# Which engine splits which block of two MLPs, the order of a Strassen product, and the PSUM banks of second layers

## The chip, the core and the metric

The program runs on one core of a Trainium2 chip. The metric is device time in microseconds (us) of one execution, as the median of three. TensorE (PE) does the matrix products; its weight loads are listed as PEld. VectorE (DVE), ScalarE (ACT) and GpSimd (POOL) do everything on elements; SyncE (SP) issues the transfers. Each engine works off its own queue in order. PE writes into PSUM, the others read it there, except GpSimd, which works on SBUF alone.

## The reference, cut to what matters

```
attn = clustered_attention(q, k, v, centroids)      # 2 batches, 8 heads, 768 tokens, 64 wide
x = attn.transpose(0, 2, 1, 3).reshape(1536, 512)
h = x @ w_in                  # first MLP, w_in 512 x 2048
g = h * sigmoid(h)
x = g @ w_out                 # 2048 x 512
gate = sigmoid(x @ w_gate)    # second MLP, w_gate and w_val 512 x 1536
val = x @ w_val
out = (gate * val) @ w_out2   # 1536 x 512
```

All is float32. Each operand of an MLP product is kept as a high and a low part, and a product is three PE products: high by high, high by low, low by high. The low part of a block is the block minus its high part.

## The kernel before

**Stages.** The attention over four pairs of heads in each of two batches takes roughly the first 275 us. The first MLP follows in N1 = 8 layers of 256 hidden columns, the second in N2 = 6. A layer of the first MLP makes its hidden block (`hidden`, "first layer" product) and adds that block times its rows of `w_out` to `acc` (`mixed`). A layer of the second MLP makes gates and values (`gated`) and adds their product times `w_out2` (`out_of`).

**One Strassen product.** `strassen` (L700) makes a 2 x 2 block product from seven half-size products, named by letters: x, y, w, z, and then X (accumulated onto x's bank), v and W (accumulated onto w's bank). It gives four result blocks: block (1,1) from u3 and w once z is done, block (0,0) from X, block (1,0) from v, block (0,1) from W. Here the first number (m) is the half of the hidden columns and the second (h) the half of the tokens. x and w sit in PSUM pool `ppa`, y, z and v in `ppb`; each pool has two banks, and a bank is handed on when its reader is done. v is the product of a22 with the operand t4.

**What follows each block.** In `hidden`, ACT applies Silu (L783), ACT writes the high part (`gha`, L61), and an engine subtracts for the low part (`gla`, L760 in `split`): GpSimd for h = 0, VectorE for h = 1. In `gated`, ACT makes the gate by Sigmoid (L835); the value block is multiplied by its gate (L841), then split into `ghb` and `glb`. In all layers of the second MLP but the last, GpSimd multiplies blocks (1,1) and (1,0) and subtracts for blocks (0,0) and (1,0); in the last layer VectorE does it all.

**The order of the work.** PE's order is that of the program text (`manual_schedule` for PE, L925). One step of `strassen` is one product. The loop (L940, L961) issues x and y of the next layer, then the second-layer product of the layer before, then the remaining five products. So PE's steady order is: w z X v W, next x, next y, second-layer product (`y_00None` to `y_21None`, or `z`), w z and so on; in the second MLP seven gate products and seven value products take the place of the seven. All other engines' orders are laid down by a planner, which walks a simulated timeline and prefers the ready instruction that stands earlier in the program text. Weight conversions stand early there: they are traced when `weights` first reaches two jobs ahead.

**Banks of second layers.** A second-layer product has six bank-size parts; `third` (L690) puts parts 0, 1, 3, 4 into `ppb` and parts 2, 5 into `ppa`. In the first and last `out_of` and in single-batch `mixed` the parts alternate.

**Weight conversions.** Each 128 x 512 block of weights takes ACT L597, POOL L598, and on VectorE L599, L600 and L601; then ACT and POOL split it (L61, L609), with POOL sums L636 to L639 for Strassen's operands.

**Start and middle.** Layer 0 of the first MLP is done per batch: `hidden(0, ONE[0])` by Strassen for batch 0, and `hidden_directly(0, 1)` without Strassen for batch 1 (products `p`), while `sums` (L82 to L100) makes the right-hand operands t1 to t4 for batch 1. Layer 0 of the second MLP is done directly for both batches (`gated_directly`, products `q` and `r`), and `sums` and `last` make the Strassen operands of the second MLP's input (tiles `yt`).

Of the kernel before, what the change touches and what calls it, by code (L numbers as in the profile page):

```python
# [15 lines left out]
ALU = mybir.AluOpType  # L16
# [15 lines left out]
def clustered_attention_then_two_mlps(ctx, tc, qT, kT, v, cen, w1i, w1o, w2g, w2v, w2o, out):  # L32
    nc = tc.nc
# [25 lines left out]
    def cast(eng, o, i):  # L59
        if eng is nc.scalar:  # L60
            return nc.scalar.activation(o, i, AF.Copy)  # L61
        if eng is nc.gpsimd:
            return nc.gpsimd.tensor_scalar(o, i, 1.0, 1.0, op0=ALU.mult, op1=ALU.mult)
        return nc.vector.tensor_copy(o, i)  # L64
# [14 lines left out]
    def right_quarter(name, b, q, caster, subber):  # L79
        right_operand(name, b, q, quarters(b)[q], caster, subber, "t1" if q == "12" else None)  # L80
# [21 lines left out]
    def right_last(name, b, src, caster, subber):  # L102
        right_operand(name, b, "t1", src, caster, subber)

    rp = ctx.enter_context(tc.tile_pool(name="rp", bufs=2))
    with ExitStack() as att:
# [182 lines left out]
        for j, (r, o) in enumerate(((L, U), (U, L))):  # L289
# [5 lines left out]
            last = dma(km[r, j].bitcast(F32), kl[r].bitcast(F32))  # L295
# [242 lines left out]
        for n in range(len(tiles) + LAG):  # L538
            if n < len(tiles):
                p, j, i = tiles[n]  # L540
# [42 lines left out]
    ppa = ctx.enter_context(tc.tile_pool(name="ppa", bufs=2, space=PSUM))  # L583
    ppb = ctx.enter_context(tc.tile_pool(name="ppb", bufs=2, space=PSUM))

    N1, N2 = M1 // 2, M2 // 2
# [91 lines left out]
    def weights(*key):  # L678

        n = place[key]  # L680
        for c in range(n, min(n + AHEAD + 1, len(jobs))):
            if c not in made:
                with tc.issue_after(ends[0].ins) if c > AHEAD else nullcontext():
                    made[c] = jobs[c]()
        return made[n]

    def bank(name, pool=None):
        return (pool or ppb).tile([P, 2, NB], F32, tag="o", name=name)

    def third(n, free=False):  # L690
        if free:
            return (ppa, ppb)[n % 2]
        return ppa if n % 3 == 2 else ppb

    def temporary(name):
        return up.tile([P, 2, HS], F32, tag="u", name=name)

    ALL = slice(0, B)

    def strassen(w, name, take, bs, order="xywzXvW"):  # L700

        def run(o, a, q, start=True):
            for k in range(KQ):
                for n, (s, t) in enumerate(((0, 0), (0, 1), (1, 0))):
                    for b in range(B)[bs]:
                        nc.tensor.matmul(  # L706
                            o[:, b, 0:HS],
                            lhsT=w[a][s][:, k, :],
                            rhs=right[b, q][t][:, k, :],
                            start=start and k == 0 and n == 0,  # L710
                            stop=k == KQ - 1 and n == 2,
                            skip_group_check=not start,
                        )
            return o[:, bs, 0:HS]

        name += f"_{bs.start}"
        add = partial(nc.vector.tensor_tensor, op=ALU.add)
        o, c = {}, {}

        def column(n):  # L720
            c[n] = temporary(f"{name}{n}")[:, bs]
            return c[n]

        for n in order:
            if n == "x":
                o[n] = bank(f"{name}x", ppa)
                nc.scalar.activation(column("u2"), run(o[n], "a11", "11"), AF.Copy)
            elif n == "y":
                add(c["u2"], run(bank(f"{name}y"), "s2", "t2"), c["u2"])
            elif n == "z":  # L730
                add(column("u3"), run(bank(f"{name}z"), "s3", "t3"), c["u2"])
            elif n == "w":
                o[n] = bank(f"{name}w", ppa)
                q = run(o[n], "s1", "t1")
            elif n == "X":
                take(run(o["x"], "a12", "21", start=False), 0, 0, bs, False)
            elif n == "v":
                nc.vector.tensor_tensor(
                    c["u3"], c["u3"], run(bank(f"{name}v"), "a22", "t4"), op=ALU.subtract
                )  # L740
                take(c["u3"], 1, 0, bs, True)
            else:
                run(o["w"], "s4", "22", start=False)
                add(c["u2"], q, c["u2"])
                take(c["u2"], 0, 1, bs, True)
            if "w" in o and "u3" in c and "d" not in c:
                add(column("d"), q, c["u3"])
                take(c["d"], 1, 1, bs, True)
            yield
# [3 lines left out]
    def split(src, m, at, i, subber):  # L753

        for t in "hl":
            if (i, m, t) not in gs:
                gs[i, m, t] = gp.tile([P, 2, B, HS], R32, tag=f"g{t}{m}", name=f"g{t}{i}_{m}")
        hi, lo = (gs[i, m, t][(slice(None), *at)] for t in "hl")
        cast(nc.scalar, hi, src)
        subber.tensor_tensor(lo, src, hi, op=ALU.subtract)  # L760
# [16 lines left out]
            take(o[:, :, 0:HS], m, b)  # L777
            yield

    def hidden(i, bs, order="xywzXvW"):  # L780
        def take(c, m, h, bs, inside):
            g = c if inside else temporary(f"g{i}_{m}{h}{bs.start}")[:, bs]
            nc.scalar.activation(g, c, AF.Silu)  # L783
            split(g, m, (h, bs), f"a{i}", nc.gpsimd if h == 0 else nc.vector)

        yield from strassen(weights("1i", i), f"h{i}", take, bs, order)

    def hidden_directly(i, b):
        def take(c, m, b):
            g = temporary(f"g{i}_{m}_{b}")  # L790
            nc.scalar.activation(g, c, AF.Silu)
            split(g, m, (slice(0, 2), b), f"a{i}", nc.vector)

        yield from direct(weights("1i", i), f"p{i}", take, b)
# [35 lines left out]
    def gated(i, bs):  # L830
        gates = {}

        def gate(c, m, h, bs, inside):
            g = c if inside else temporary(f"g2{i}_{m}{h}{bs.start}")[:, bs]
            nc.scalar.activation(g, c, AF.Sigmoid)  # L835
            gates[m, h] = g

        def value(c, m, h, bs, inside):
            g = gates[m, h]
            beside = nc.gpsimd if i < N2 - 1 else nc.vector  # L840
            (beside if inside and m else nc.vector).tensor_tensor(g, c, g, op=ALU.mult)  # L841
            split(g, m, (h, bs), f"b{i}", beside if h == 0 else nc.vector)

        yield from strassen(weights("2g", i), f"g{i}", gate, bs)
        yield from strassen(weights("2v", i), f"v{i}", value, bs)

    def gated_directly(i, b):
        gates = {}

        def gate(c, m, b):  # L850
            gates[m] = temporary(f"g2{i}_{m}_{b}")
            nc.scalar.activation(gates[m], c, AF.Sigmoid)

        def value(c, m, b):
            g = gates[m]
            nc.vector.tensor_tensor(g, c, g, op=ALU.mult)
            split(g, m, (slice(0, 2), b), f"b{i}", nc.vector)

        yield from direct(weights("2g", i), f"q{i}", gate, b)
        yield from direct(weights("2v", i), f"r{i}", value, b)  # L860
# [35 lines left out]
    def steps(main, beside=iter(()), n=None):  # L896

        for _ in main:
            next(beside, None)
            if n is not None:  # L900
                n -= 1
                if n == 0:
                    return

    def run(gen):
        for _ in gen:
            pass
# [4 lines left out]
    def plain_operands(name, b):  # L912
        for q in ("11", "21", "12", "22"):
            right_quarter(name, b, q, ACT, DVE)
            yield

    def sums(name, b):
        return right_sums(temporary, name, b, ACT, DVE, kept)

    def last(name, b):  # L920
        right_last(name, b, kept.pop(b), ACT, DVE)

    ONE = [slice(b, b + 1) for b in range(B)]

    order = tc.manual_schedule(engines={mybir.EngineType.PE})  # L925
# [3 lines left out]
        right_quarter("x", 1, q, POOL, POOL)  # L929
    for q in ("21", "22"):  # L930
        right_quarter("x", 1, q, ACT, DVE)
    run(hidden(0, ONE[0], "xwyXzvW"))
    beside = sums("x", 1)
    steps(hidden_directly(0, 1), beside)
    run(beside)
    last("x", 1)
    run(mixed(0, 0))
    run(mixed(0, 1))
    run(hidden(1, ALL))
    for i in range(2, N1):  # L940
        following = hidden(i, ALL) if i < N1 - 1 else hidden(i, ONE[0], "xyXzwvW")
        steps(following, n=2 if i < N1 - 1 else 4)
        run(mixed(i - 1))
        run(following)
    run(hidden(N1 - 1, ONE[1]))
    run(mixed(N1 - 1, 0))
    beside = plain_operands("y", 0)
    steps(mixed(N1 - 1, 1), beside)
    run(beside)
    beside = plain_operands("y", 1)  # L950
    steps(gated_directly(0, 0), beside)
    run(beside)
    beside = sums("y", 0)
    steps(gated_directly(0, 1), beside)
    run(beside)
    run(sums("y", 1))
    last("y", 0)
    last("y", 1)
    run(out_of(0))
    run(gated(1, ALL))  # L960
    for i in range(2, N2):  # L961
        following = gated(i, ALL)
# [57 lines left out]
```

## Time and profile before

| | before |
|---|---|
| median of 3 runs | 893.11 us (892.16 to 893.66) |
| the profiled execution | 893.1 us, span 891.3 us, mean granted TensorE clock 0.959 |
| PE busy | 809.5 us (91%) |
| DVE busy | 644.4 us (72%) |
| POOL busy | 407.9 us (46%) |
| ACT busy | 387.5 us (43%) |
| chain that ended last | PE 55%, DVE 23%, POOL 12%, issue 3%, ACT 3%, DMA 3% |

The profiled execution's time lies 1.8 us over its span and agrees with the median. Busy shares are means over unlike stages: the question is always which wait ends last just before PE goes on. The chain of work that ended last is followed back from the last instruction and says which engine held the end at each moment.

### The profile page before, as it was taken

To read this page: it belongs to the slowest core of one execution; us is meant where nothing else is said; L and a number is where in the kernel's file an instruction comes from. 1 tells how busy PE (TensorE), PEld (TensorE's weight loads), DVE (VectorE), ACT (ScalarE), POOL (GpSimd) and SP (SyncE) were. 2 spreads that over 40 slices of the span, in tenths; PEclk is the share of its full clock that TensorE was granted. 3 is DMA by queue.
4 is the path that set the end of the run, shared out by engine and by line. 5 is a ranking of instruction groups with operands and counts; after the bars stand their busy time and mean duration, and the time that the engine had idled before them with its cause. 6 is when DMAs were issued, how large, how long until landed. Compare 5 with 4: busy or idle time off the path is not lost.

```text
span 891.3 us, 12033 instructions
## 1 busy us (share of the span) xinstructions
PE 809.5 (91%) x4592; PEld 701.4 (79%) x4592; DVE 644.4 (72%) x824; ACT 387.5 (43%) x667; POOL 407.9 (46%) x358
## 2 busy tenths in 40 slices
PE   6899999999998998898898999998979799797987
PEld 4777777777677997787777889997968779686886
DVE  5778877887996988665666669994665858758453
ACT  3456556555675572432514326554424314243030
POOL 3511360581444684534626335552665726558100
PEclk7899999999999999999999999999989999898998
DMA  7564465356321123112111212201210112201003
GB/s 213 143 161 109 113 163 137 89 148 166 108 66 39 57 95 105 41 67 71 47 48 48 71 47 71 96 24 48 71 68 28 71 48 72 71 25 48 1 1 141
DMA packets 25042, 72.10 MB, mean 81 GB/s; under 512 B 4100, under 2 KB 4184, under 8 KB 24984
## 3 DMA queue, kind: packets, MB, share of 16 engines
q1 hardware_dynamic: 24984, 71.33, 26.9%
q8 instruction: 36, 0.59, 0.3%
q14 instruction: 22, 0.18, 0.1%
HBM read 47.87 MB, written 3.19 MB: 57 GB/s over the span
## 4 chain that ended last, share of the span: by engine, by line
PE 55%; DVE 23%; POOL 12%; issue 3%; ACT 3%; DMA 3%; SPq 0%; ACTq 0%; POOLq 0%; DVEq 0%
PE z L879 11%; PE s L412 5%; PE v L452 5%; PE t L444 3%; DVE nm L420 3%; PE g_0w L706 2%; DVE acc L800 2%; PE pm L149 2%; PE y_01None L820 2%; PE y_21None L820 2%; POOL glb L760 2%; PE y_20None L820 2%; PE y_11None L820 2%; PE y_10None L820 2%; PE h_0w L706 2%
## 5 line engine op out<-in xcount | busy, mean ns | idle before, releaser
L425 ACT ACTIVATE e<-s,nm 128x768 f32<-128x768 f32 x96 | 86.5, 902 | 66.8 <-DVE nm L420 65.7
L879 PE MATMUL z<-wu,ghb 128*128 128x512 f32 x288 | 96.9, 420 | 11.5 <-ACT ghb L61 11.5
L420 DVE TENSOR_REDUCE nm<-s 128x1 f32<-128x768 f32 x96 | 90.8, 949 | 11.9 <-PE s L412 9.2
L879 PEld LDWEIGHTS z<-wu,ghb 128*128 128x128 f32 x288 | 58.6, 206 | 26.1 <-ACT ghb L61 14.0
L452 PE MATMUL v<-ph,vv 128*64 128x256 f32 x576 | 75.6, 388 | 0.9 <-DVE xf L464 0.6
L879 PE MATMUL z<-wu,glb 128*128 128x512 f32 x144 | 61.3, 426 | 15.4 <-POOL glb L760 10.9
L800 DVE TENSOR_TENSOR acc<-z,acc 128x1024 f32<-128x1024 f32 x30 | 36.7, 1224 | 41.1 <-PE z L879 41.1
L412 PE MATMUL s<-ka,qa 128*128 128x384 f32 x192 | 59.6, 392 | 6.0 <-ACT e L425 6.0
L444 PE MATMUL t<-ident,e 128*128 128x128 f32 x384 | 58.4, 281 | 2.6 <-ACT ph L61 1.6
L452 PEld LDWEIGHTS v<-ph,vv 128*64 128x64 f32 x576 | 37.8, 136 | 23.9 <-issue 5.9
L412 PE MATMUL s<-k,q 128*128 128x384 f32 x192 | 51.8, 351 | 1.0 <-DVE k L329 1.0
L444 PEld LDWEIGHTS t<-ident,e 128*128 128x128 f32 x384 | 45.3, 144 | 8.5 <-ACT ph L61 1.9
L879 PEld LDWEIGHTS z<-wu,glb 128*128 128x128 f32 x144 | 29.4, 204 | 25.0 <-POOL glb L760 13.3
L412 PEld LDWEIGHTS s<-ka,qa 128*128 128x128 f32 x192 | 29.9, 195 | 20.9 <-ACT e L425 12.5
L350 POOL TENSOR_SCALAR qq<-qq 128x768 f32<-128x768 f32 x7 | 6.1, 874 | 82.5 <-DMA qq<-in_qT 67.2
L439 PE MATMUL u<-ident,e 128*128 128x128 f32 x192 | 36.7, 281 | 0.2 <-DVE ph L64 0.2
L61 ACT ACTIVATE ph<-t 128x512 f32<-128x512 f32 x48 | 28.6, 596 | 19.0 <-PE t L444 18.7
L412 PEld LDWEIGHTS s<-k,q 128*128 128x128 f32 x192 | 35.3, 194 | 1.6 <-DVE k L329 1.5
L482 POOL TENSOR_TENSOR acc<-xf,rb 128x768 f32<-128x768 f32 x7 | 12.8, 1826 | 52.0 <-DVE xf L464 35.1
L464 DVE TENSOR_TENSOR xf<-v,other 64x256 f32<-64x256 f32 x48 | 20.1, 418 | 22.1 <-ACT other L461 21.9
L64 DVE COPY ph<-t 128x512 f32<-128x512 f32 x48 | 32.6, 679 | 4.7 <-PE t L444 4.6
L64 DVE COPY ph<-u 128x512 f32<-128x512 f32 x48 | 32.5, 678 | 3.1 <-PE u L439 3.1
(635 smaller groups left out, 2254.9 us busy)
## 6 DMA issues: line engine op xcount, KB each, us to landing
ri<-in_w1i SPq DMA_DIRECT2D x16, 512.0 KB, 3.2
ro<-in_w1o SPq DMA_DIRECT2D x16, 512.0 KB, 3.1
ka<-kh SPq DMA_DIRECT2D x32, 192.0 KB, 3.9
rg<-in_w2g SPq DMA_DIRECT2D x12, 512.0 KB, 3.1
rv<-in_w2v SPq DMA_DIRECT2D x12, 512.0 KB, 3.1
ru<-in_w2o SPq DMA_DIRECT2D x12, 512.0 KB, 3.2
qq<-in_qT SPq DMA_DIRECT2D x8, 384.0 KB, 4.7
kk<-in_kT SPq DMA_DIRECT2D x8, 384.0 KB, 5.5
```

The costliest lines, as they stand in the source:

```text
L61: return nc.scalar.activation(o, i, AF.Copy)
L64: return nc.vector.tensor_copy(o, i)
L412: nc.tensor.matmul(s[:, g, 0:HS], lhsT=a[:, j, i * P : (i + 1) * P], rhs=c[:, j, g * HS : (g + 1) * HS], start=n == 0, stop=n == 1,)
L420: nc.vector.tensor_reduce(nm, s[:, :, 0:HS], axis=AX.XY, op=ALU.max, negate=True)
L425: nc.scalar.activation(e, s[:, :, 0:HS], AF.Exp, bias=nm, scale=1.0, accum_out=tots[p][:, n : n + 1])
L439: nc.tensor.transpose(both[:, kt - 4, i % GT, :], e[:, kt * P : (kt + 1) * P], ident)
L444: nc.tensor.transpose(t[:, kt, :], e[:, kt * P : (kt + 1) * P], ident)
L452: nc.tensor.matmul(o[(L, U)[kt % 2]], lhsT=vv[:, j, kt, :], rhs=ph[:, kt, :], start=kt < 2, stop=kt >= NT - 2,)
L706: nc.tensor.matmul(o[:, b, 0:HS], lhsT=w[a][s][:, k, :], rhs=right[b, q][t][:, k, :], start=start and k == 0 and n == 0, stop=k == KQ - 1 ...
L800: nc.vector.tensor_tensor(z, o, z, op=ALU.add)
L820: nc.tensor.matmul(o[:, d, 0:width], lhsT=s[:, d, k, :], rhs=t[:, c], start=k == 0 and m == 0, stop=k == 1 and m == 2,)
L879: nc.tensor.matmul(o[:, a, :], lhsT=s[:, q * P : (q + 1) * P], rhs=r, start=k == 0 and m == 0, stop=k == 1 and m == 2,)
```

## The change

- `third`: parts 0 and 3 of a second-layer product go to `ppa`, the other four to `ppb`.
- The Strassen order "xywzXvW" becomes "xywzvXW": v stands before X. At layer 0's batch 0, "xwyXzvW" becomes "xwXyzvW", and the first half of `hidden_directly(0, 1)` stands before its last product W.
- `hidden`: GpSimd subtracts for block (1,1) alone, VectorE for the other three.
- `gated`: GpSimd multiplies and subtracts for block (1,1) alone, VectorE for the others, in every layer.
- Between the MLPs: `sums` and `last` of batch 0 stand ahead of `gated_directly(0, 1)`, those of batch 1 behind it.

```diff
     def third(n, free=False):
         if free:
             return (ppa, ppb)[n % 2]
-        return ppa if n % 3 == 2 else ppb
+        return ppb if n % 3 else ppa
...
-    def strassen(w, name, take, bs, order="xywzXvW"):
+    def strassen(w, name, take, bs, order="xywzvXW"):
...
-    def hidden(i, bs, order="xywzXvW"):
+    def hidden(i, bs, order="xywzvXW"):
         def take(c, m, h, bs, inside):
             g = c if inside else temporary(f"g{i}_{m}{h}{bs.start}")[:, bs]
             nc.scalar.activation(g, c, AF.Silu)
-            split(g, m, (h, bs), f"a{i}", nc.gpsimd if h == 0 else nc.vector)
+            split(g, m, (h, bs), f"a{i}", nc.gpsimd if m and h else nc.vector)
...
         def value(c, m, h, bs, inside):
             g = gates[m, h]
-            beside = nc.gpsimd if i < N2 - 1 else nc.vector
-            (beside if inside and m else nc.vector).tensor_tensor(g, c, g, op=ALU.mult)
-            split(g, m, (h, bs), f"b{i}", beside if h == 0 else nc.vector)
+            eng = nc.gpsimd if m and h else nc.vector
+            eng.tensor_tensor(g, c, g, op=ALU.mult)
+            split(g, m, (h, bs), f"b{i}", eng)
...
-    run(hidden(0, ONE[0], "xwyXzvW"))
+    front = hidden(0, ONE[0], "xwXyzvW")
+    steps(front, n=6)
+    following = hidden_directly(0, 1)
+    next(following)
+    run(front)
     beside = sums("x", 1)
-    steps(hidden_directly(0, 1), beside)
+    next(beside)
+    steps(following, beside)
     run(beside)
...
-    beside = sums("y", 0)
-    steps(gated_directly(0, 1), beside)
-    run(beside)
+    run(sums("y", 0))
+    last("y", 0)
+    run(gated_directly(0, 1))
     run(sums("y", 1))
-    last("y", 0)
     last("y", 1)
```

## Rows read from the trace of the kernel before

**Rows 1.** Waits of PE from 277 us on: total us, times, longest us.

```profile
PE y_00None L820 <- POOL gla L760: 15.8, 5, 3.4
PE z L879 <- ACT ghb L61: 11.5, 5, 2.7
PE z L879 <- POOL glb L760: 10.9, 4, 2.9
PE h_0w L706 <- DVE acc L800: 6.6, 5, 1.3
PE g_0w L706 <- DVE acc L800: 5.3, 4, 1.3
PE z L879 <- DVE glb L760: 4.5, 2, 3.4
PE h_0w L706 <- DVE h_0d L747: 2.3, 1, 2.3
PE h_0y L706 <- ACT ci L597: 1.6, 1, 1.6
```

**Rows 2.** Chain that ended last, around `mixed(4)`: start us, us, work.

```profile
443.99 2.48 POOL gla L760
446.51 3.43 PE y_00None L820 x8
...
452.70 2.72 PE y_10None L820 x12
...
464.90 2.35 PE h_0w L706 x12
467.25 2.08 PE h_0z L706 x12
```

**Rows 3.** Stretches of 2 us in `out_of(4)`: PE busy, granted clock, DMA.

```profile
821.60:823.60 2.00, 1.97 (x5) 0.50 0.00 0
...
825.60:827.60 2.00, 2.00 (x11) 1.00 0.00 0
```

**Rows 4.** Whole layers, first and second MLP: busy PE, PEld, DVE, ACT, POOL; clock.

```profile
446.51:484.06 37.55, 32.83 (x157) 28.93 (x157) 23.69 (x25) 12.56 (x19) 17.42 (x17) 0.95 0.17 57
...
712.04:766.99 54.95, 48.39 (x240) 43.76 (x240) 37.00 (x38) 17.60 (x26) 31.64 (x29) 0.93 0.17 58
```

**Rows 5.** Timelines of ACT, DVE and POOL, first MLP's layer 5: start us, us.

```profile
477.66 0.83 ACT L61 ACTIVATE gha<-h_0u 128x768 fp32r<-128x768 f32 x1
...
474.40 2.32 DVE L601 SCALAR_TENSOR_TENSOR ci<-ri,ci 128x512 int32<-128x512 int32 x1
...
481.49 2.51 POOL L760 TENSOR_TENSOR gla<-h_0u,gha 128x768 fp32r<-128x768 f32 x1
```

**Rows 6.** Chain that ended last, `out_of(3)`.

```profile
766.99 17.03 PE z L879 x67
```

**Rows 7.** Tiles `glb` and line 841 by form: duration ns minimum, median, maximum.

```profile
L760 DVE TENSOR_TENSOR glb<-g_0d,ghb x5: 950/2550/2556, 646.4 to 864.7; 128x768 fp32r<-128x768 f32 x5
...
L841 POOL TENSOR_TENSOR g_0d<-v_0d,g_0d x4: 2034/2042/2228, 642.9 to 808.4; 128x768 f32<-128x768 f32 x4
```

**Rows 8.** Timeline of DVE, values of the second MLP's layer 2.

```profile
697.97 1.17 DVE L599 TENSOR_SCALAR cu<-cu 128x512 int32<-128x512 int32 x1
...
699.92 1.47 DVE L600 SCALAR_TENSOR_TENSOR cu<-ru,cu 128x512 int32<-128x512 int32 x1
701.43 2.22 DVE L601 SCALAR_TENSOR_TENSOR cu<-ru,cu 128x512 int32<-128x512 int32 x1
```

**Rows 9.** Timeline of PE, `out_of(5)`.

```profile
867.45 0.74 PE L879 MATMUL z<-wu,ghb 128*128 128x512 f32 x2 [1.60 <-ACT ghb L61]
```

**Rows 10.** Timeline of DVE, between the MLPs.

```profile
583.54 0.95 DVE L87 TENSOR_TENSOR yt<-acc 128x768 f32<-128x768 f32 x1
...
621.56 0.96 DVE L729 TENSOR_TENSOR g_0u<-g_0y,g_0u 128x768 f32<-128x768 f32 x1 [11.51 <-PE g_0y L706]
```

**Rows 11.** Timeline of DVE, start of the first MLP.

```profile
303.37 2.04 DVE L760 TENSOR_TENSOR gla<-g,gha 128x768 fp32r<-128x768 f32 x1
```

## The prediction

> **What bounds the kernel now.** Start with PE's busy share: at 91% it looks full, so the question is what the other 9% is and whether the 91% runs at full clock. From 277 us on, the list of PE's waits answers the first half [rows 1]: 58.5 us in 27 waits, and nearly all have one of two shapes. The first lies at the start of each second-layer product: PE stops for a low part that GpSimd still makes (`gla`, five times, 3.4 us the longest; in the second MLP first for the high part `ghb`, then for `glb`). The second stands at the next product w: nine times 1.3 us for VectorE's read of the last part (`acc`, L800), that is, for a PSUM bank. The chain that ended last shows both as links on the path [rows 2]: GpSimd's subtraction, then the product, then w. The reader should also see what follows the first wait: eight matmuls take 3.43 us where twelve take 2.72 otherwise, so 1.6 us go to slow matmuls. The granted clock says why: 0.50 after such a wait (1.2 GHz), 1.00 four us later (2.4 GHz) [rows 3]. In `out_of(3)` 67 matmuls take 17.03 us instead of 67 x 2.72 / 12 = 15.2: 1.8 us lost the same way [rows 2, 6]. So a wait of about 3 us costs nearly 5.
>
> Whole layers confirm it. Work per layer is 7 products of 2.08 us and 72 matmuls of 2.72 / 12 us, 14.56 + 16.32 = 30.88 us, where the layer takes 37.55: 6.67 lost. In the second MLP 14 x 2.08 + 16.32 = 45.44 against 54.95: 9.51 lost [rows 2, 4]. VectorE is busy 23.7 of the 37.55 and 37.0 of the 54.95, GpSimd 17.4 and 31.6 [rows 4]: neither is full on average; what counts is order.
>
> **Why the first block is late.** Block (1,0) comes from v. ACT has its high part at 477.66 + 0.83 = 478.49, but GpSimd, whose queue holds weight work in front, begins the subtraction at 481.49 and takes 2.51 us [rows 5]. VectorE does the same in 0.95 us when undisturbed [rows 7].
>
> **The change, part by part.** All sums are against the profiled 893.1 us (span 891.3 and 1.8 around it), which agrees with the median 893.11.
>
> *Banks.* With parts 0 and 3 in `ppa`, w follows part 3 in its pool, not part 5; part 3 is read two parts (5.4 us) earlier, so the wait of 1.3 us goes. w took 2.35 us, not 2.08, after it [rows 2], so each of the nine waits is worth about 1.6: 5 x 1.6 = 8.0 in the first MLP; the four in the second lie inside the 9.51. In return part 0 now needs w's bank, so it waits for VectorE's L744, and z, v and the parts keep `ppb`, whose readers are done sooner.
>
> *First MLP.* GpSimd loses two subtractions per layer and gains (1,1), which is ready four products before the second-layer product starts; VectorE gains one on balance, about 0.95 us in 30.9, and v comes 2.08 us earlier. The five waits (15.8), four slow starts (4 x 1.6 = 6.4) and the five bank waits (8.0) are 30.2 us. What is late next? I laid out VectorE's queue from v's end with one conversion in it, as now. The second-layer product starts 4 x 2.08 = 8.3 us after v. L738, the last conversion step (2.32 contended [rows 5]), two subtractions and L744 at 0.95 are 6.1 us plus about 1 of waiting for ACT: it fits, with some 1.2 us to spare. The other new wait is X. Its bank goes to the next x, which used to start two products after X and now starts one product after: ACT has 2.08 us for a Silu of 0.8 that may stand behind another Silu or high part. Bounds 0 to 2.5 us per layer; I take 0.5, near the rows of ACT, whose steps are 0.8 each [rows 5], for six layers: 3.0. Gain 27.2.
>
> *Second MLP, layers 1 to 4.* Upper bound 4 x 9.51 = 38.0. VectorE gains two instructions on balance (L841 and L760 of (1,0), L760 of (0,0), less L760 of (1,1)). Here VectorE is tighter. Between v's end and the next x lie 2 x 2.08 = 4.16 us, and in them it must do L738, L841 of (1,0) and L841 of (0,0), 2.85 us. But a conversion runs there now: 1.17 + 1.47 + 2.22 = 4.86 us [rows 8]. If its first two steps come in front of X's reader, 2.85 + 2.64 = 5.5, so the next x waits 1.4 us; then L601, two subtractions and L744 end about 0.8 us after the second-layer product could start. That is 2.2 us per layer, with bounds 0 (no conversion in front) and 5.4 (both subtractions at the contended 2.55 [rows 7] as well). I take 2.2, since the planner put that conversion there in this trace, and 0.3 for X's bank between gates and values (ACT, five layers): 8.8 + 1.5 = 10.3. Gain 27.7. GpSimd's two instructions for (1,1), 2.04 [rows 7] and at most 2.51 us [rows 5], start four products before they are needed first and are wanted only in the fourth part: covered; without that cover they would cost what they cost now.
>
> *Last layer.* No next x and y cover its blocks. Its two waits are 1.6 for `ghb` [rows 9] and 1.1 (4.5 less 3.4) for `glb` [rows 1], and 1.8 for the clock: 4.5. After the change (0,0), from X, comes last: L841, high part, L760 is about 2.7 us after X, while W covers 2.08. So 0.7 to 1 stays: gain 3.4, bounds 2 to 4.5.
>
> *Between the MLPs.* In `out_of(0)` PE waits 3.4 us for VectorE's `glb` [rows 1], plus 1.8 of clock. VectorE there runs the sums of both batches from 583.54 on, ahead of batch 1's values, though it is idle 11.5 us later before 621.56 [rows 10]. Putting batch 0's sums first and batch 1's behind the values moves work into that hole. Gain 4.5, bounds 0 and 5.2.
>
> *Start.* X in place of y fills part of the 1.6 us wait at y (one half-size product, 1.0), and the first direct product covers the 2.3 us wait at W: 3.3. But the second part of batch 1's `gla` is only done at 303.37 + 2.04 [rows 11], because VectorE is behind with sums; if that doesn't move, PE waits there instead. I take 1.5, bounds -2 and 3.3.
>
> Sum: 27.2 + 27.7 + 3.4 + 4.5 + 1.5 = 64.3; 893.1 - 64.3 = **828.8**, forecast 829 us. With every new wait at zero: 893.1 - (30.2 + 38.0 + 4.5 + 5.2 + 3.3) = 811.9.
>
> **Rivals.**
>
> *VectorE and GpSimd in each other's way.* The row of `glb` on VectorE has a minimum of 0.95 and a median of 2.55 us [rows 7], so a subtraction here can cost 1.6 more when GpSimd works at the same time. The change gives VectorE more of them. At 2.55 for both moved ones, the first MLP loses 2 x 1.6 less the 1.2 to spare, 2.0 per layer, and the second 3.2: 829 + 5 x 2.0 + 4 x 3.2 = **852**. For it: the row; and (1,1)'s work on GpSimd falls into the same window. Against: GpSimd does less there than before. The Trainium skill, page "SBUF — State Buffer", section "Who interferes with whom", says that a VectorE instruction with two SBUF inputs contends with a GpSimd instruction that reads SBUF, and whoever comes second is held for the whole of the other. The doubled row fits that, and by that rule this rival is the one to expect whenever a weight instruction of GpSimd starts first.
>
> *The moved work doesn't come earlier.* The change is meant to have the blocks ready in time, but the planner may leave the moved subtractions behind conversions, so that the wait at the second-layer product keeps its length under VectorE's name. Then the banks (8.0 + 4 x 1.6), the last layer, the middle and the start are left: 893.1 - 14.4 - 9.4 = **869**. Against: VectorE's totals leave room [rows 4].
>
> *Slower.* X's bank becomes the stop. Place: the next x in the second MLP, and part 0's bank behind L744 in the first. With one conversion at its long durations and L841 at 2.55, X's reader ends 0.95 + 4.86 + 2.55 + 0.95 = 9.3 us after v against 4.16: a wait of 5.15, with the clock 6.95, still under 9.51. It decides with a second conversion in the same window: 6.95 + 4.86 = 11.8, over 9.51; in the first MLP 0.95 + 9.72 + 5.1 + 0.95 = 16.7 against 8.3, with the clock 10, over 6.67. Then 893.1 + 4 x 2.3 + 5 x 3.3 - 9.4 = **909**. Against: the rows show one conversion in that window [rows 8].
>
> **How the numbers follow.** Forecast 829: 0.68, its own range 812 to 843. Port rival 852: 0.17. Work not earlier, 869: 0.08. Slower, 909: 0.05. No change: 0.02. The range to hold 8 in 10 runs from 812 to 857: it takes in the forecast and most of the port rival and leaves out the rest. A measurement of this kernel can tell about 0.2% (1.8 us) from no change. Faster 0.93, same 0.02, slower 0.05.
>
> **What would show it.** Right: no wait of PE for GpSimd's `gla` or `glb`; no wait of w for `acc`; layers of about 31.4 and 48 us; clock 1.00 through second-layer products; new short waits of x for ACT in the first MLP and for L841 in the second, about 0.5 and 1.4 us. Wrong: a wait of `y_00None` or `z` of over 2 us for VectorE's L760 or L744 with the clock at 0.50 behind it, VectorE subtractions at 2.55 throughout, or batch 1's `gla` holding up the first `mixed`.

## The result and the profile after

The changed kernel takes 834.75 us (median of four, 832.95 to 835.97) where the kernel before takes 893.28: a ratio of 0.9345 (95% interval 0.9325 to 0.9366), that is, 6.5% faster. The forecast was 829 us. In a second run of the changed kernel the ratio was 0.9349 (0.9331 to 0.9368). The profiled execution took 835.97 us, span 834.2. One execution of one kernel below (X ahead of v in the value product) took 1975.92 us; its ratio is that of the other three.

PE's waits from 277 us on, in the changed kernel (us in total, times, longest), against [rows 1]:

```profile
PE z L879 <- DVE glb L760: 7.0, 4, 2.0
PE g_0x L706 <- DVE g L841: 5.1, 4, 1.8
PE y L820 <- DVE gla L760: 3.3, 2, 2.5
PE y_00None L820 <- DVE gla L760: 1.6, 2, 0.9
PE h_1w L706 <- DVE h_1d L747: 1.4, 1, 1.4
PE z L879 <- ACT ghb L61: 0.3, 1, 0.3
PE h_0x L706 <- ACT h_0u L727: 0.2, 1, 0.2
```

No wait names GpSimd any more, and none names `acc`; 58.5 us (59.0 with two waits of 0.3 and 0.2 us that [rows 1] leave out) have become 18.9. The largest two are new ones, both on VectorE in the second MLP. Whole layers (first and second MLP; columns as in [rows 4]):

```profile
365.30:396.24 30.94, 30.94 (x158) 28.12 (x157) 26.02 (x26) 12.80 (x20) 17.13 (x16) 1.00 0.20 69
717.75:766.55 48.80, 46.05 (x241) 42.55 (x241) 37.42 (x41) 17.16 (x26) 29.32 (x28) 1.00 0.19 65
```

In a steady layer of the first MLP PE is busy for all of 30.94 us: the bare work was 30.88, so nothing is left to gain there. In the second, 48.80 us stand against 45.44 of bare work. The granted clock is 1.00 in both. The chain that ended last shows the same; the first two lines answer [rows 2], the last (of `out_of(2)`) answers [rows 6]:

```profile
443.67 2.10 PE h_0w L706 x12
...
458.25 2.74 PE y_00None L820 x12
...
666.87 1.49 DVE glb L760
668.35 1.42 DVE g_0u L841
669.77 1.41 DVE glb L760
671.22 16.16 PE z L879 x70
```

w follows the second-layer product without a gap and takes 2.10 us instead of 2.35; twelve matmuls of `y_00None` take 2.74 us, no slow ones among them; 70 matmuls of z take 16.16, that is 0.23 us each, where 67 took 17.03. What is left on the chain is three VectorE instructions in a row in front of z.

Where the time went, from the starts of PE's products in the two timelines (us):

| stretch | before | after | difference | forecast |
|---|---|---|---|---|
| attention, to the first product of the first MLP | 269.7 | 267.7 | -2.0 | 0 |
| from there to `mixed(1)` | 62.2 | 62.8 | +0.6 | -1.5 |
| `mixed(1)` to `mixed(6)` | 185.7 | 158.9 | -26.7 | -27.2 |
| `mixed(6)` to `out_of(0)` | 77.6 | 78.7 | +1.1 | 0 |
| `out_of(0)` | 21.9 | 16.8 | -5.1 | -4.5 |
| second MLP's layers 1 to 4, to `out_of(5)` | 247.9 | 225.3 | -22.6 | -27.7 |
| `out_of(5)` | 21.3 | 18.9 | -2.4 | -3.4 |
| sum | | | -57.1 | -64.3 |

The attention's 2 us are scatter between executions: the same changed kernel ended it at 268.7 in another execution, and in the traces of the kernels here it ends between 266.5 and 270.7 us. Each column is one execution, and other rows scatter too: in the second profile of the changed kernel `mixed(1)` to `mixed(6)` takes 157.2 us and `out_of(5)` 20.5, so a difference of under 2 us in one row shows little by itself.

### The profile page after: what moved, and what is told of

Its sections match the earlier page's. It is cut to its first block, busy times and chain, and to the rows that moved or that the text cites. A ratio compares the mean times of both kernels' runs of the same rounds, so it can differ in the third digit from the quotient of the medians.

```text
span 834.2 us, 12042 instructions
## 1 busy us (share of the span) xinstructions
PE 792.6 (95%) x4592; PEld 693.8 (83%) x4592; DVE 657.0 (79%) x839; ACT 386.9 (46%) x667; POOL 398.0 (48%) x343
## 4 chain that ended last, share of the span: by engine, by line
PE 64%; DVE 28%; issue 3%; ACT 3%; DMA 1%; POOL 1%; SPq 0%; ACTq 0%; DVEq 0%; POOLq 0%
PE z L879 11%; PE s L412 6%; PE v L452 5%; DVE nm L420 3%; PE t L444 3%; PE h_0x L706 3%; PE h_0w L706 3%; PE g_0w L706 3%; PE pm L149 2%; DVE ph L64 2%; PE y_00None L820 2%; PE y_01None L820 2%; PE y_20None L820 2%; PE y_11None L820 2%; PE y_10None L820 2%
## 5 line engine op out<-in xcount | busy, mean ns | idle before, releaser
L879 PE MATMUL z<-wu,ghb 128*128 128x512 f32 x288 | 88.9, 390 | 0.3 <-ACT ghb L61 0.3
L879 PEld LDWEIGHTS z<-wu,ghb 128*128 128x128 f32 x288 | 53.9, 188 | 11.4 <-ACT ghb L61 0.7
L879 PE MATMUL z<-wu,glb 128*128 128x512 f32 x144 | 56.6, 393 | 7.1 <-DVE glb L760 7.0
L879 PEld LDWEIGHTS z<-wu,glb 128*128 128x128 f32 x144 | 27.0, 188 | 14.7 <-DVE glb L760 9.3
L61 ACT ACTIVATE ph<-t 128x512 f32<-128x512 f32 x48 | 28.6, 596 | 18.9 <-PE t L444 18.7
L64 DVE COPY ph<-t 128x512 f32<-128x512 f32 x48 | 32.5, 678 | 4.7 <-PE t L444 4.6
L64 DVE COPY ph<-u 128x512 f32<-128x512 f32 x48 | 32.5, 677 | 2.0 <-PE u L439 1.9
```

The costliest lines, as they stand in the source:

```text
L879: nc.tensor.matmul(o[:, a, :], lhsT=s[:, q * P : (q + 1) * P], rhs=r, start=k == 0 and m == 0, stop=k == 1 and m == 2,)
```

## The experiments

Ratios are against the kernel before on the same chip, with their 95% intervals. A gain in us is the ratio's, taken of 893.28 us; in the runs of single parts its interval is 3 to 6 us to either side.

### The parts one by one

**Banks alone.**

```diff
-        return ppa if n % 3 == 2 else ppb
+        return ppb if n % 3 else ppa
```

> The kernel before with the new banks of second-layer products alone. Theory (each part of the change takes away its own wait): the nine waits of w for the last part's read are gone, 9 x 1.6 us with the refill, so 893.1 - 14.4 = about 879 us; the waits for GpSimd's low parts stay at 3.4 us in the first MLP. Rival (the bank wait only hides a later one): part 0 now waits for the bank that W's reader L744 gives back, or w's time is given back at the next low part, so that the sum is under 5 us: 888 or more.

Measured: 881.27 us, ratio 0.9834 (0.9779 to 0.9889), so 1.7% or 14.8 us (10 to 20). Its waits of PE:

```profile
PE y_00None L820 <- POOL gla L760: 15.5, 5, 3.4
PE z L879 <- ACT ghb L61: 10.5, 5, 2.2
PE z L879 <- POOL glb L760: 8.1, 4, 2.7
...
PE z L879 <- DVE v_0u L744: 1.7, 3, 0.9
```

The waits for `acc` are gone and those for `gla` stay, as the theory has it. The rival's mechanism exists as well, but small: part 0 now waits 1.7 us in all for the bank that L744 gives back, in the second MLP (`z`). This trace holds something unexpected about the clock, below.

**Order alone.**

```diff
-    def strassen(w, name, take, bs, order="xywzXvW"):
+    def strassen(w, name, take, bs, order="xywzvXW"):
...
-    def hidden(i, bs, order="xywzXvW"):
+    def hidden(i, bs, order="xywzvXW"):
```

> The kernel before with v ahead of X in the Strassen order alone; GpSimd keeps its blocks. Theory (the engine's queue, not the product's place, makes the block late): block (1,0) was ready for its subtraction 3 us before GpSimd began it, so 2 us more of lead gain little: 0 to 8 us, 885 to 893 us, waits for gla and glb of GpSimd stay. Rival (the order is the cure): the waits for gla fall by 2 us each and the clock stays up: 893 - 5 x 3.5 - 5 x 4 = about 855 us.

Measured: 879.33 us, ratio 0.9810 (0.9745 to 0.9876): 17 us, twice the most that the theory allowed. Its waits for `gla` at `mixed(1)` and `mixed(2)`, from PE's timeline (the bracket is the wait before the instruction):

```profile
335.98 0.79 PE L820 MATMUL y_00None<-gla,wo 128*128 128x512 f32 x1 [2.99 <-POOL gla L760]
372.49 0.50 PE L820 MATMUL y_00None<-gla,wo 128*128 128x512 f32 x1 [1.47 <-POOL gla L760]
```

One layer of the first MLP in the same kernel (columns as in [rows 4]):

```profile
439.00:473.30 34.30, 31.51 (x158) 28.00 (x157) 22.26 (x25) 12.70 (x20) 16.84 (x17) 1.00 0.19 62
```

From the second layer on the wait is 1.47 us instead of 3.4, and behind it the first matmul takes 0.50 us, not 0.79, with the clock at 1.00 through the layer: the layer falls from 37.55 to 34.3. So the product's place does matter for the first MLP while GpSimd keeps its blocks, and GpSimd still ends the wait; neither theory had the size.

**GpSimd's share alone.** Only the lines of `hidden` and `value` that pick the engine are changed.

```diff
-            split(g, m, (h, bs), f"a{i}", nc.gpsimd if h == 0 else nc.vector)
+            split(g, m, (h, bs), f"a{i}", nc.gpsimd if m and h else nc.vector)
...
-            beside = nc.gpsimd if i < N2 - 1 else nc.vector
-            (beside if inside and m else nc.vector).tensor_tensor(g, c, g, op=ALU.mult)
-            split(g, m, (h, bs), f"b{i}", beside if h == 0 else nc.vector)
+            eng = nc.gpsimd if m and h else nc.vector
+            eng.tensor_tensor(g, c, g, op=ALU.mult)
+            split(g, m, (h, bs), f"b{i}", eng)
```

> The kernel before with the new share of GpSimd alone; the order stays, X ahead of v. Theory (the engine is what matters): in the first MLP the waits for gla go wholly with the clock's dips, 22 us; in the second about 25 of the 31.7 us go, since v's block is 2 us later than in the changed kernel but the next x has no wait for X's reader: 845 to 852 us. Rival (VectorE is full in that stretch, so the block is as late as before under VectorE's name): 870 us or more, with waits of z for VectorE's glb of 3 us and the clock at 0.50 behind them.

Measured: 855.86 us, ratio 0.9556 (0.9506 to 0.9606): 39.7 us, the largest part, but 4 us short of the theory's end. Its waits:

```profile
PE z L879 <- DVE glb L760: 12.8, 6, 2.6
...
PE h_1w L706 <- DVE h_1d L747: 1.1, 1, 1.1
```

Of the first MLP's second-layer products only the first two still wait for `gla` (0.4 us, and 1.6 at `mixed(1)`); in the second MLP z waits 2.1 to 2.6 us for VectorE in each layer but the last (1.1). So VectorE's queue is late there too, by less than GpSimd's was: between theory and rival.

**The middle alone.** Batch 0's sums and `last` move ahead of batch 1's direct product.

```diff
-    beside = sums("y", 0)
-    steps(gated_directly(0, 1), beside)
-    run(beside)
+    run(sums("y", 0))
+    last("y", 0)
+    run(gated_directly(0, 1))
     run(sums("y", 1))
-    last("y", 0)
```

> The kernel before with batch 0's sums moved ahead of gated_directly(0, 1) alone. Theory: the wait of z for VectorE's glb in out_of(0) goes with the slow clock behind it, 3.4 + 1.8 = 5.2 us: 888 us. Rival (the gain in the middle needs the other parts, since VectorE is behind from the first MLP's end): the same as before, 893 us.

Measured: 890.87 us, ratio 0.9948 (0.9919 to 0.9977), 4.6 us. `out_of(0)` takes 17.1 us instead of 21.9. The part stands alone, as the theory said.

Together the four alone give 14.8 + 17 + 39.7 + 4.6 = 76 us, the whole change 58. Between `mixed(1)` and `mixed(6)` they give 6.6, 9.9 and 21.2 (banks, order, share), 37.7 in all, against 26.7 for the whole: three cures of losses that together end at the bare work. In the second MLP, from `out_of(1)` to the last matmul, they give 6.9, 5.5 and 15.4, 27.8 in all, against 28.8: there they add up (in the changed kernel's second profile the stretch gave 26.0), and something is still left.

One part has nothing left to do beside another. With GpSimd's share alone the steady layers of the first MLP take 32.5 us:

```profile
400.05:432.58 32.53, 31.21 (x157) 28.02 (x157) 23.94 (x26) 12.59 (x19) 16.51 (x16) 1.00 0.20 65
```

The 1.6 us above the bare work is the wait for the bank, and none for a low part is left that the order could shorten. The whole change without its order was not run; the next section undoes the order in the value product alone.

### What is left in the second MLP

VectorE's timeline in the values of layer 2, changed kernel, answers [rows 8]:

```profile
660.10 0.94 DVE L738 TENSOR_TENSOR v_0u<-v_0u,v_0v 128x768 f32<-128x768 f32 x1
660.97 1.47 DVE L601 SCALAR_TENSOR_TENSOR cv<-rv,cv 128x512 int32<-128x512 int32 x1
662.36 1.36 DVE L841 TENSOR_TENSOR g_0u<-v_0u,g_0u 128x768 f32<-128x768 f32 x1
663.64 0.94 DVE L841 TENSOR_TENSOR g<-v_0x,g 128x768 f32<-128x768 f32 x1
664.51 0.94 DVE L744 TENSOR_TENSOR v_0u<-v_0w,v_0u 128x768 f32<-128x768 f32 x1
665.37 1.57 DVE L599 TENSOR_SCALAR cu<-cu 128x512 int32<-128x512 int32 x1
666.87 1.49 DVE L760 TENSOR_TENSOR glb<-g_0u,ghb 128x768 fp32r<-128x768 f32 x1
668.27 1.50 DVE L841 TENSOR_TENSOR g_0u<-v_0u,g_0u 128x768 f32<-128x768 f32 x1
669.69 1.48 DVE L760 TENSOR_TENSOR glb<-g,ghb 128x768 fp32r<-128x768 f32 x1
```

X's reader, the second L841, ends at 664.58, behind a conversion step (L601): the next x starts 1.08 us late. Then the subtraction that z needs first (`glb<-g`, block (0,0)) stands behind another conversion step, the subtraction of (1,0) and the multiplication of block (0,1), which z needs only in its fourth part. The next runs take this apart.

**X ahead of v in the value product.**

```diff
-        yield from strassen(weights("2v", i), f"v{i}", value, bs)
+        yield from strassen(weights("2v", i), f"v{i}", value, bs, "xywzXvW")
```

> The changed kernel with the old order (X ahead of v) in the value product of the second MLP alone, so that the next x has two products of time for X's reader again. Theory (VectorE's queue is what is late, and the wait at x is one of two places where it shows): the waits of g_0x for L841 (5.1 us in all) go, and the wait of z for VectorE's glb grows by about as much, since all the same instructions must be through: layers of 48 to 49.5 us as now (48.8), total within 4 us of 835. Rival (the wait at x is a loss of its own, made by the order): layers of about 47.4 us, 5.5 us less in all, 829 us.

Measured: 833.63 us, ratio 0.9296 (0.9271 to 0.9322). The time alone doesn't decide between the two; the same kernel ran once more for its trace:

> The changed kernel with X ahead of v in the value product alone, once more, for its trace. Theory (one queue, two places): no wait of g_0x for L841, a wait of z for VectorE of 2.5 to 3.3 us instead of 1.66, layers of 48 to 49.5 us. Rival: waits of z as now and layers of about 47.4 us.

Measured: 835.02 us, ratio 0.9329 (0.9299 to 0.9359). Its waits of z:

```profile
PE z L879 <- DVE glb L760: 10.5, 5, 2.4
```

One layer of the second MLP in the same kernel:

```profile
669.16:717.34 48.18, 45.78 (x242) 42.59 (x242) 37.40 (x41) 17.05 (x26) 29.39 (x27) 1.00 0.20 66
```

No wait of g_0x for L841 is left in its list, z waits up to 2.4 us (the theory said 2.5 to 3.3) instead of 1.66, and the layer takes 48.2 instead of 48.8. So the wait at x is mostly one of two places where the same late queue shows; its own share is 0.6 us a layer. By that much the change's order is a small loss in the value product; in the gate product it was not tried apart.

**Less of the conversions.** L600 and L601 are left out for value and output weights from layer 1 on, so this kernel doesn't compute the reference's result.

```diff
+        if name[0] not in "uv" or name[1] == "0":
             nc.vector.scalar_tensor_tensor(ti, low, 29, ti, op0=ALU.logical_shift_right, op1=ALU.bitwise_or)
             nc.vector.scalar_tensor_tensor(ti, up_, SIGN, ti, op0=ALU.bitwise_and, op1=ALU.bitwise_or)
```

> The changed kernel without L600 and L601 of the weight conversions of the second MLP's value and output weights from layer 1 on (two of VectorE's three instructions of each; the weights are then not those of the reference). Theory (a conversion standing in VectorE's queue between L738 and X's reader makes the waits of x and z): the waits of g_0x for L841 go, those of z for glb fall under 0.7 us, a layer takes 45.5 to 46.5 us instead of 48.8, total about 835 - 4 x 2.8 = 824 us. Rival (GpSimd's port work slows VectorE's own multiplications and subtractions from 0.95 to 1.5 us and that makes the waits): layers of 47.5 us or more.

Measured: 824.47 us, ratio 0.9199 (0.9153 to 0.9244). Its waits at x and z (lines stand one further down here), and then one layer:

```profile
PE g_0x L707 <- DVE g L842: 2.2, 3, 1.2
PE z L880 <- DVE glb L761: 2.0, 1, 2.0
```

```profile
664.78:711.08 46.30, 45.81 (x241) 42.64 (x241) 30.56 (x34) 17.05 (x26) 27.38 (x27) 1.00 0.22 69
```

The layer falls to 46.3 us, inside the theory's bounds; z waits only in the last layer. The wait at x is more than halved (5.1 to 2.2 in all), not gone: in layer 2 a conversion step (L599, 1.23 us) and the multiplication of (1,0) (1.49 us) still stand in front of X's reader. The run doesn't single out the conversions for z, though: the planner also laid the multiplication of (0,1) behind the subtraction of (0,0) here (VectorE starts them at 664.72 and 662.32 us), which the next run does by itself.

**The first low part first.** The multiplication of block (0,1) is queued behind the subtraction of block (0,0); `split` now returns its subtraction, which is kept in `done`.

```diff
-            eng.tensor_tensor(g, c, g, op=ALU.mult)
-            split(g, m, (h, bs), f"b{i}", eng)
+            with tc.issue_after(done[0, 0].ins) if h > m else nullcontext():
+                eng.tensor_tensor(g, c, g, op=ALU.mult)
+            done[m, h] = split(g, m, (h, bs), f"b{i}", eng)
```

> The changed kernel with one instruction of VectorE moved: in the value product the multiplication of block (0,1), needed only in the fourth part of the second-layer product, is queued behind the subtraction of block (0,0), needed in the first. Theory (the wait of z is the queue's order: L841 of (0,1) took 1.5 us in front of the subtraction that z waits for): the wait of z for glb falls from 1.66 to about 0.2 us, a layer takes 47.0 to 47.6 us instead of 48.8, the whole 5 to 7 us less, about 829 us. Rival (z's wait is set by GpSimd holding the port, or by ACT's high part): the wait stays over 1.2 us and the time within 2 us of 835.

Measured: 829.67 us, ratio 0.9266 (0.9232 to 0.9300). VectorE's timeline at the same place (L842 is the multiplication here), and then one layer:

```profile
665.66 1.49 DVE L760 TENSOR_TENSOR glb<-g_0u,ghb 128x768 fp32r<-128x768 f32 x1
667.07 1.49 DVE L760 TENSOR_TENSOR glb<-g,ghb 128x768 fp32r<-128x768 f32 x1
668.49 1.48 DVE L842 TENSOR_TENSOR g_0u<-v_0u,g_0u 128x768 f32<-128x768 f32 x1
```

```profile
667.71:715.13 47.42, 46.04 (x241) 42.55 (x241) 36.66 (x41) 17.08 (x26) 29.39 (x27) 1.00 0.20 67
```

One instruction changes places; z waits 0.28 us instead of 1.66 in layers 2 to 4, and a layer takes 47.4 us, as expected. GpSimd's work was the same, so the rival's forecast (a wait of over 1.2 us) fails: the order is enough to cure z's wait, though each of the three instructions still takes about 1.49 us instead of 0.95. The wait at x stays at 1.1.

**The last layer on VectorE alone.** GpSimd gets nothing for i = N2 - 1.

```diff
-            eng = nc.gpsimd if m and h else nc.vector
+            eng = nc.gpsimd if m and h and i < N2 - 1 else nc.vector
```

> The changed kernel, but in the last layer of the second MLP VectorE multiplies and subtracts for block (1,1) too. Theory (VectorE and GpSimd hold each other up: L841 and L760 took 1.61 and 1.89 us beside GpSimd's two instructions, 0.95 alone): VectorE gains two instructions of 0.95 and loses 1.6 us of being held, so the last wait of z, 2.0 us, stays within 0.7 us of that: same time, within 1 us of 835. Rival (GpSimd's share is a true relief): the last wait grows by 1.9 us or more.

Measured: 836.27 us, ratio 0.9335 (0.9310 to 0.9360), the same as the changed kernel. The waits of `out_of(5)` are 0.93 and 0.77 us instead of 0.34 and 2.00. Its length, 18.88 us, equals that in the changed kernel's first profile (18.89), but in the second, with the same waits, it is 20.53: the clock fell there behind the wait of 2.0 us. Every L841 and L760 of VectorE in that stretch takes 0.95 or 0.96 us here, where two took 1.61 and 1.89 beside GpSimd's two instructions. So GpSimd's help with one block costs VectorE 1.6 us and saves it two instructions of 0.95: nearly nothing, in this layer, where GpSimd has no weights to prepare.

### The start, and a better version

**The start as before.** The changed kernel with the edits of layer 0's start taken back.

```diff
-    front = hidden(0, ONE[0], "xwXyzvW")
-    steps(front, n=6)
-    following = hidden_directly(0, 1)
-    next(following)
-    run(front)
+    run(hidden(0, ONE[0], "xwyXzvW"))
     beside = sums("x", 1)
-    next(beside)
-    steps(following, beside)
+    steps(hidden_directly(0, 1), beside)
```

> The changed kernel with the start of the first MLP as before (batch 0's last product and the direct product of batch 1 in their old places, X behind y). Theory (VectorE's sums and conversions set the start, not the two waits of PE): from the first product of the first MLP to layer 1 the stretch is 43.5 us as in the kernel before instead of 44.1: nothing gained or lost by the new start, within 1.5 us. Rival (the new start saves the 3.3 us of PE's two waits): the stretch is 46 to 47 us and the whole 2 to 3 us slower, about 838 us.

Measured: 833.69 us, ratio 0.9300 (0.9269 to 0.9332); the time alone is not clear of the changed kernel's (0.9325 to 0.9366). To layer 1's first product the stretch is 43.9 us (44.1 in the changed kernel), to `mixed(1)` 62.6 (62.8): nothing gained or lost, as the theory has it. But `mixed(1)` to `mixed(2)` takes 31.1 us here, 34.7 in the changed kernel's profile and 32.9 in that of its second run: `y_00None` waits twice for `gla`, 1.6 us in all, and in the first of the two profiles the clock fell behind it. The other kernels with the new start take 32.9 to 33.1 us there, the one other with the old start 31.5. So the new start costs about 2 us, with the clock's fall 3.6, one layer further on.

PE doesn't come to `mixed(1)` any sooner; VectorE's queue is laid out differently. In the changed kernel two conversion steps stand right in front of the first subtraction that `mixed(1)` needs:

```profile
327.49 1.54 DVE L599 TENSOR_SCALAR ci<-ci 128x512 int32<-128x512 int32 x1
329.07 1.67 DVE L600 SCALAR_TENSOR_TENSOR ci<-ri,ci 128x512 int32<-128x512 int32 x1
330.66 0.95 DVE L760 TENSOR_TENSOR gla<-g,gha 128x768 fp32r<-128x768 f32 x1
```

`mixed(1)` begins at 330.58, so this subtraction starts 0.1 us too late; with the old start the conversion steps stand ahead of L744, and it starts 1.6 us before `mixed(1)` does. Why the planner laid the two differently stays open.

**Three edits together.** X ahead of v in the value product, the multiplication of (0,1) behind the subtraction of (1,0), and the old start (its diff stands above).

```diff
-            eng.tensor_tensor(g, c, g, op=ALU.mult)
-            split(g, m, (h, bs), f"b{i}", eng)
+            with tc.issue_after(done[1, 0].ins) if h > m else nullcontext():
+                eng.tensor_tensor(g, c, g, op=ALU.mult)
+            done[m, h] = split(g, m, (h, bs), f"b{i}", eng)
...
-        yield from strassen(weights("2v", i), f"v{i}", value, bs)
+        yield from strassen(weights("2v", i), f"v{i}", value, bs, "xywzXvW")
```

> The changed kernel with three edits: X ahead of v in the value product, the multiplication of block (0,1) queued on VectorE behind the subtraction of (1,0), and the start of the first MLP as before the change. Theory (one queue, and only what stands in front of the needed instruction counts): no wait of g_0x, a wait of z of about 0.9 us instead of 2.4, layers of 46.7 us instead of 48.8 (4 x 2.1), the start 1 to 3 us less: 824 to 827 us. Rival (the order on VectorE is filled up by conversions, so the wait stays at 2 us or more): layers of 48 us, 832 us or more.

Measured: 825.77 us, ratio 0.9224 (0.9201 to 0.9247), with the changed kernel at 836.63 us on the same chip:

> The changed kernel once more, on the same chip as the combined one: 835 us within 2, layers of 48.8 us.

The combined kernel's waits of z for VectorE's `glb`, and one layer of it:

```profile
PE z L880 <- DVE glb L760: 3.2, 4, 1.0
```

```profile
663.62:710.39 46.77, 45.78 (x241) 42.58 (x241) 36.49 (x41) 16.95 (x26) 29.42 (x27) 1.00 0.20 68
```

The layer takes 46.8 us, no x waits, and z waits up to 1.0: 10.9 us less than the changed kernel, from the order of instructions alone. It beats both kernels.

## Why the prediction was right, point by point

**Banks: right.** Nine waits of w are gone; alone they were worth 14.8 us (10 to 20), forecast 14.4. That the two are so close is partly luck: in the first MLP the trace shows 6.6 us of the 8.0, 0.1 to 2.9 a layer, because the clock behind the wait for `gla` fell differently from layer to layer (below). Cleaner is the 1.6 us a layer between GpSimd's share alone (32.5) and the changed kernel (30.9), as forecast. Part 0's new wait for L744 appears (1.7 us in the run with the banks alone) and not in the changed kernel.

**First MLP: right, with two sizes off that cancel.** 26.7 us against 27.2 (28.5 in the changed kernel's second profile), so the close agreement is luck. The steady layers have no new wait at all (30.94 us), so the 0.5 us per layer taken for X's bank was too much; ACT reads X in time. Instead `mixed(1)` kept a loss of 3.8 us (34.7; 2.0 in the second profile), because VectorE's queue after the new start holds two conversion steps in front of its first subtraction. The early v, which the prediction counted among the cures, was not needed beside GpSimd's share.

**Second MLP: right mechanism, sizes too small.** The step was the layout of VectorE's queue from v's end: 1.4 us at the next x and 0.8 at z. Measured 1.08 and 1.66, in the place and behind the very kind of instruction named: a conversion step ahead of X's reader, and the subtractions behind. Two terms were missing: the multiplication of (0,1), which the planner put in front of the last needed subtraction (moving it took 1.4 us off the wait), and the duration of VectorE's own instructions: beside GpSimd they take about 1.5 us, not 0.95, which the prediction had only in its bound (2.55). Then layer 1 lost 3.7 us more (37.0 us from its first product to `out_of(1)`, 33.3 before), because its wait at x was 1.84 us and the clock fell behind it; in the second profile the clock stayed up and 2.2 were lost. Sum: 22.6 instead of 27.7, five of the seven us that the forecast is off.

**The port rival: half of it happened.** VectorE's `glb` has medians of 1.36 and 1.49 us in the changed kernel, not 2.55 [rows 7] and not 0.95. Its price was 23 us; the runs show it as part of the 5 us missed. The run with the last layer on VectorE alone isolates it there: 0.95 without GpSimd, 1.61 and 1.89 with it. The Trainium skill, page "SBUF — State Buffer", section "Who interferes with whom", says that a VectorE instruction with two SBUF inputs contends with a GpSimd instruction that reads SBUF. Those numbers agree: the two slowed ones have two SBUF inputs and overlap GpSimd's, while X's reader, with one input from PSUM, keeps 0.94. In layers 1 to 4 its share stays open. In the listing of layer 2 above, the six instructions from L601 on that took over 0.95 us (L599 takes 0.41 and L601 0.69 where GpSimd is idle) ran 4.0 us longer together than alone; that is an estimate from these rows, and more than the 2.7 us that PE waits there. Shorter instructions might then have cured those waits as well as the new order does; no run takes GpSimd out of these layers.

**Middle: right** (5.1 us against 4.5). **Last layer: its wait was mis-sized.** Its gain is 2.4 us in the first profile and 0.8 in the second, against 3.4 with a lower bound of 2 (the prediction's own terms, 4.5 less 0.7 to 1, make 3.5 to 3.8). The waits hardly shrank: 2.3 us are left of 2.7, not 0.7 to 1. The prediction saw only the chain of (0,0) itself; in VectorE's queue the subtraction of (1,0), held to 1.89 us by GpSimd, and L744 stand in front of its subtraction, and even without GpSimd 1.7 us of waits stay. The 2.4 are mostly luck: in the first profile the clock stayed up behind the wait.

**Start: no gain, and a loss behind it.** The forecast took 1.5 us of gain with a bound of -2, and named the condition and the sign of being wrong: batch 1's `gla` has to come earlier. Counted from the first product of the first MLP it ended at 34.7 us instead of 35.7, which is not enough (PE waits for it 0.8 and 2.5 us at the first `mixed`), so PE's two waits only moved. By itself the new start changes 0.2 us up to `mixed(1)`; the 2 us lost behind it were not foreseen.

**End of the first MLP: not in the forecast.** A new wait of 1.4 us at `h_1w`, in its last layer, covers the 1.1 us lost between `mixed(6)` and `out_of(0)`: VectorE's L747 stands behind conversion steps of 1.73 and 1.01 us there, and the share of GpSimd alone makes it too (1.1 us).

**Moved work not earlier; slower:** neither occurred. The moved subtractions stand behind one or two conversion steps, not behind whole conversions.

## What to carry to other kernels

When a helper engine feeds the critical product, give it the block that is ready first and is needed last, and read the queue of the engine that inherits the rest instruction by instruction: VectorE was busy 77% of a layer of the second MLP (37.4 of 48.8 us) and still made PE wait twice in it. After moving work, look at which instruction in that queue the waiting product needs, and put those it needs later behind it; here that was worth 5 us by moving one instruction, and 11 with three edits of order. Gains of several cures of one stretch add up only until the bare work is reached.

## What the runs showed that was not expected

- **The clock doesn't follow from the length of the wait before it.** In the kernel before, every wait of about 3.4 us in the first MLP's steady layers had 0.50 behind it. With the banks alone, the same waits of 3.4 us are followed by full clock at `mixed(2)`, by a fall some matmuls later at `mixed(3)` (eight take 2.74 us instead of 2.14) and by the slow clock at once from `mixed(4)` on. The first matmul after the wait takes 0.50 us at 2.4 GHz and 0.80 at 1.2; PE's timeline of that run:

```profile
366.52 0.50 PE L820 MATMUL y_00None<-gla,wo 128*128 128x512 f32 x1 [3.43 <-POOL gla L760]
401.19 0.50 PE L820 MATMUL y_00None<-gla,wo 128*128 128x512 f32 x1 [3.41 <-POOL gla L760]
437.43 0.80 PE L820 MATMUL y_00None<-gla,wo 128*128 128x512 f32 x1 [3.41 <-POOL gla L760]
```

  In the changed kernel, a wait of only 1.84 us at layer 1's x is followed by a fall, and one of 1.66 us at z is not; PE's busy time and granted clock in stretches of 2 us, and last the stretch behind the wait of 2.0 us in `out_of(5)`:

```profile
616.00:618.00 2.00, 1.81 (x9) 0.86 0.24 94
618.00:620.00 2.00, 2.00 (x8) 0.50 0.00 0
...
671.20:673.20 2.00, 1.98 (x9) 1.00 0.00 0
...
813.05:815.05 2.00, 2.00 (x9) 1.00 0.00 0
```

  In the second profile of the same kernel the two change places: the wait at layer 1's x (1.90 us) is not followed by a fall, and that in `out_of(5)` (1.99 us) is:

```profile
812.05:814.05 2.00, 2.00 (x5) 0.59 0.00 0
```

  Why one and not the other stays open. For a forecast it means that a slow start is possible behind waits of 2 us and likely, not certain, behind 3.4, and that its 1.6 us shouldn't be booked for each wait.
- **Helping can cost the helped.** GpSimd's two instructions for one block made two of VectorE's take 1.61 and 1.89 us instead of 0.95, so in the last layer the division of work gained nothing in time.
